# Second-layer chunks regrouped so that each one's output rows lie at one stride and go out in one store

## The chip, the cores and the metric

One core of a Trainium2 chip runs the whole program. The metric is device time in microseconds. The kernel before takes 325.49 us, the median of 3 runs (324.9 to 325.58).

## The reference

Eight batches with 8 heads each, 576 tokens per head, head size 64. A Nystrom attention (32 landmarks, each the mean of 18 consecutive tokens) is followed by two dense layers:

```python
A  = sm(q, k_lm);  Bm = sm(q_lm, k_lm);  C = sm(q_lm, k)
for _ in range(6): Z = 2 * Z - Z @ Bm @ Z
x  = (A @ Z @ C @ v)          # to [4608 tokens, 512]
h  = x @ w_in                 # 512 -> 2048
out = (h * sigmoid(h)) @ w_out  # 2048 -> 512, float32
```

## The kernel before, in words

A planner (class `Plan`) takes operations with priorities, dependencies and estimated durations, simulates the five engines, and writes one fixed order per engine; each engine then runs its list in that order and waits on semaphores. The order comes only from those estimates. SP's list holds the DMA transposes (`qT<-qk` at L479, four per batch from batch 2 on; `ct<-ce` at L717, two per batch from batch 2 on) and all output stores (L871). GpSimd's list issues the loads.

A token of a batch is numbered 18 l + j, with l from 0 to 31 (the landmark it belongs to) and j from 0 to 17. On the chip the 576 tokens of a batch lie as 18 blocks of 32: block x holds the 32 tokens of one j, first all nine even j, then all nine odd j (`jof`, L876: j = 2 (x mod 9) + x div 9). So the tile `etn` (the normalised attention factor, two groups of 128 rows by 576 columns) has its columns in two halves of 288.

Per batch, `layer1` (L789) folds w_in into a matrix `m`, so that the hidden layer is `m` times `etn`: for each of 16 pieces of the hidden dimension two matmuls over 512 token columns (L800) and one Silu on ScalarE into `gm` (L809). The last 64 token columns (blocks 16 and 17, that is j = 15 and 17) go separately: 16 small matmuls per eight pieces (L821) into one bank, and one Silu into `gx` (L831), which collects two batches, 128 tokens.

`layer2` (L842) takes 128 tokens at a time as a chunk: four pieces of four matmuls over w_out into one bank (L850), a copy to one of three buffers `ost` on ScalarE or VectorE (L862), and the store (L864), whose `stores` function issues the DMAs. `layer2_batch` (L879) makes four chunks per batch from `gm` and, after each odd batch, one chunk from `gx` (called the x chunk here). The first matmuls of an attention batch that use `ct`, the transposed third softmax, are at L730 (`cv0`, then `cv1`); at L707 the first two batches make `ct` on TensorE instead.

A store has to write 32 rows per j. In a chunk with j = 0, 2, 4, 6 the destination is 4 pieces by 32 rows by 512 numbers. The third chunk of each batch holds j = 16, 1, 3, 5, which are not at one step, so `stores` issues a DMA of 32 rows and one of 96. The x chunk issues one DMA for each of its two batches, each 2 pieces (j = 15, 17) by 32 rows. That makes five DMAs per batch and two more per pair of batches, 48 in all.

Of the kernel before, what the change touches and what calls it, by code (L numbers as in the profile page):

```python
# [9 lines left out]
AF = mybir.ActivationFunctionType  # L10
# [231 lines left out]
def act_us(n):  # L242
    return 0.06 + 0.00083 * n
# [6 lines left out]
def mm_us(n, count=1):  # L250
    return count * max(n / 2400 + 0.0025, 0.028)
# [3 lines left out]
def kernel(  # L255
# [9 lines left out]
    nc = tc.nc  # L265
    B, H, S, Dh = q.shape
    L = 32
    J = S // L
    JP = J // 2
# [20 lines left out]
    def bank(o, i=0):  # L290
        return banks[o.slot[i]]

    def ring(pool, shape, dt, nm, n):
        return [pool.tile(shape, dt, tag=f"{nm}{i}", name=f"{nm}{i}") for i in range(n)]
# [17 lines left out]
    etn_r = ring(smp, [128, NG, S], BF, "etn", 2)  # L312
# [4 lines left out]
    m_r = ring(smp, [128, NG, DFF], BF, "m", 2)  # L317
# [4 lines left out]
    def mm(out_ap, lhsT, rhs, start=True, stop=True):  # L322
        nc.tensor.matmul(out=out_ap, lhsT=lhsT, rhs=rhs, start=start, stop=stop,  # L323
                         skip_group_check=True)
# [76 lines left out]
    def consts(e):  # L401
# [13 lines left out]
        out=idb, in_=idb, compare_op=OP.is_equal, fill=0.0, base=0, pattern=[[-1, 128]],  # L415
# [371 lines left out]
    l2_last = {}  # L787

    def layer1(b):  # L789
        m_sb, etn = m_r[b % 2], etn_r[b % 2]  # L790
        gm, gx = gm_r[b % 3], gx_r[(b // 2) % 2]
        gm_ops[b], gx_ops[b] = [], []
        pes = []
        for dc in range(NDC):
            cell = {}

            def hm(e, dc=dc, cell=cell):
                ps = bank(cell["o"])
                for g in range(NG):
                    mm(ps, m_sb[:, g, dc * 128:(dc + 1) * 128], etn[:, g, 0:512],  # L800
                       start=(g == 0), stop=(g == 1))
            p = 1000.0 + 100 * b + dc
            o = cell["o"] = A(f"h{dc}.{b}", [("PE", mm_us(512, 2))], hm,
                              etn_ops[b] + m_ops[b, dc // 4] + l2_last.get(("m", b - 3), []), p,
                              psum=1, cls="L1")
            pes.append(o)
            o.unit = b
            gm_ops[b].append(A(f"g{dc}.{b}", [("ACT", act_us(512))],
                               lambda e, dc=dc, cell=cell: nc.scalar.activation(  # L809
                                   out=gm[:, dc, :], in_=bank(cell["o"]), func=AF.Silu),  # L810
                               [o], p, table="silu").reads(o))
            gm_ops[b][-1].unit = b
            if dc % 8 == 7:
                d0 = dc - 7
                cell = {}

                def xm(e, d0=d0, cell=cell):
                    ps = bank(cell["o"]).rearrange("p (c x) -> p c x", c=8)
                    for d in range(8):
                        for g in range(NG):  # L820
                            mm(ps[:, d], m_sb[:, g, (d0 + d) * 128:(d0 + d + 1) * 128],  # L821
                               etn[:, g, 512:576], start=(g == 0), stop=(g == 1))
                o = cell["o"] = A(f"hx{d0}.{b}", [("PE", mm_us(64, 16))], xm,
                                  etn_ops[b] + m_ops[b, dc // 4]
                                  + l2_last.get(("x", b // 2 - 2), []), p + 0.5, psum=1, cls="L1")
                pes.append(o)
                o.unit = b
                c = (b % 2) * 64
                gx_ops[b].append(A(
                    f"gx{d0}.{b}", [("ACT", act_us(512))],  # L830
                    lambda e, d0=d0, cell=cell, c=c: nc.scalar.activation(  # L831
                        out=gx[:, d0:d0 + 8, c:c + 64],
                        in_=bank(cell["o"]).rearrange("p (c x) -> p c x", c=8), func=AF.Silu),
                    [o], p + 0.5, table="silu").reads(o))
                gx_ops[b][-1].unit = b
        l1_done[b] = A(f"l1done.{b}", [("SP", 0.0)], lambda e: None, pes, 0.0, lag=0.0)
# [5 lines left out]
    def layer2(src, deps, prio, stores, split=False):  # L842
        head = [None]
        prev_piece = None
        pieces = []
        for qt in range(4):
            def lm2(e, qt=qt):
                ps = bank(head[0])
                for dc in range(4 * qt, 4 * qt + 4):
                    mm(ps, src(dc), w_out_sb[:, dc, :], start=(dc == 0), stop=(dc == NDC - 1))  # L850
            d = deps(qt) + ([prev_piece] if qt else []) + [wo_ops[qt]]
            d = [(x, 0.0) if x is prev_piece else x for x in d]
            o = A(f"o{qt}@{prio}", [("PE", mm_us(512, 4))], lm2, d, prio + 0.01 * qt,
                  psum=0 if qt else 1, cls="L2")
            if qt == 0:
                head[0] = o
            prev_piece = o
            pieces.append(o)
        i = nost[0] % 3
        nost[0] += 1  # L860
        ost = ost_r[i]
        c = A(f"oc@{prio}", either(512), lambda e: copy(e, ost, bank(head[0])),  # L862
              [prev_piece, ost_st.get(i)], 900.0 + prio / 100).reads(head[0])
        st = A(f"os@{prio}", [("SP", 0.15)], lambda e: stores(ost), [c], prio, dma=0.65, lag=1.6)  # L864
        ost_st[i] = st
        return pieces

    def store_rows(b, js, ost, p0):
        n = len(js)
        step = js[1] - js[0] if n > 1 else 1  # L870
        return nc.sync.dma_start(  # L871
            out=out[b * S:(b + 1) * S, :].rearrange("(l j) n -> j l n", j=J)
            [js[0]:js[-1] + 1:step],
            in_=ost[p0:p0 + n * L, :])

    def jof(blk):  # L876
        return 2 * (blk % JP) + blk // JP

    def layer2_batch(b):  # L879
        l2_last["m", b] = []  # L880
        for c in range(4):
            js = [jof(x) for x in range(4 * c, 4 * c + 4)]

            def stores(ost, js=js):
                i = 0
                while i < 4:
                    n = 1
                    while i + n < 4 and js[i + n] == js[i] + 2 * n:
                        n += 1
                    r = store_rows(b, js[i:i + n], ost, i * L)  # L890
                    i += n
                return r
            l2_last["m", b] += layer2(
                lambda dc, c=c: gm_r[b % 3][:, dc, c * 128:(c + 1) * 128], lambda qt: gm_ops[b][4 * qt:4 * qt + 4],
                5000.0 + 100 * b + 10 * c, stores)
        if b % 2 == 1:
            def stores(ost):
                for bb in range(2):
                    r = store_rows(b - 1 + bb, [jof(16), jof(17)], ost, 64 * bb)
                return r  # L900
            l2_last["x", b // 2] = layer2(
                lambda dc: gx_r[(b // 2) % 2][:, dc, :], 
                lambda qt: [gx_ops[b - 1][qt // 2], gx_ops[b][qt // 2]],
                5000.0 + 100 * b + 40, stores)
# [7 lines left out]
    for b in range(B):  # L912
        attn(b)
        layer1(b)
        layer2_batch(b)
# [4 lines left out]
    with tc.manual_schedule(engines={ET.PE, ET.Activation, ET.DVE, ET.Pool, ET.SP}):  # L920
        table = None
        for o, e, t, end, switch in order:
# [4 lines left out]
            r = o.emit(e)  # L927
# [39 lines left out]
```

## Time and profile before

| | |
|---|---|
| median of 3 runs | 325.49 us |
| the profiled execution, its own time | 326.66 us |
| span of its instructions | 324.9 us |
| mean granted TensorE clock | 0.917 of full speed |
| TensorE matmul busy | 271.2 us (83%) |
| ScalarE busy | 178.1 us (55%) |
| VectorE busy | 97.3 us (30%) |
| GpSimd busy | 106.2 us (33%) |
| chain of waits by engine | PE 48%, DMA 32%, POOL 7%, SP's queue 5% |

Times in the profile's rows are microseconds from the start of the span. PE is TensorE, PEld its weight loads, ACT ScalarE, DVE VectorE, POOL GpSimd, SP the engine that issues transposes and stores; a q behind the name means the engine's instruction queue. "Busy" of PE is not PE at its peak. PEclk is the granted clock as a share of 2.4 GHz, so 0.50 is 1.2 GHz. The DMA share of a stretch is the mean busy share of the core's 16 DMA engines, so 0.125 is two of them; packets still in flight at the end of a short stretch can push it above 1.

### The profile page before, as it was taken

The numbers are of one execution on the slowest core, as the hardware profiler recorded it, in microseconds if no ns is written. First come the engines' busy times: TensorE is split into PE (matmuls) and PEld (weight loads), VectorE is DVE, ScalarE is ACT, GpSimd is POOL, SyncE is SP. The second block draws the span as 40 slices with busy tenths as digits, with TensorE's granted clock in tenths as the row PEclk, the third lists the DMA queues.
The fourth block names the chain that finished last, engine by engine and source line by source line (L and its number), as shares of the span: only waits on it lengthen the run. The fifth ranks groups of instructions, "written<-read, shape, count | busy, mean of one in ns | idle before, by whom it ended". The sixth has DMA issues, their size and how long they took to land.

```text
span 324.9 us, 5951 instructions
## 1 busy us (share of the span) xinstructions
PE 271.2 (83%) x2367; PEld 135.5 (42%) x2367; DVE 97.3 (30%) x258; ACT 178.1 (55%) x405; POOL 106.2 (33%) x133
## 2 busy tenths in 40 slices
PE   7999999669889069998991599979199999999950
PEld 6975554234444034444430345434044544444420
DVE  1685055301736214036460150445125200000000
ACT  1887983838628326984591199835149792111120
POOL 7166249328503570395329222930000000000000
PEclk9999999959999858999996599999669999999995
DMA  6999997894497939787792479778811011322221
GB/s 117 208 200 206 204 209 123 143 202 65 82 155 138 164 62 125 138 148 146 128 217 67 74 136 183 95 95 151 91 32 34 3 32 32 68 68 81 80 76 48
DMA packets 58148, 37.60 MB, mean 116 GB/s; under 512 B 39177, under 2 KB 49417, under 8 KB 58121
## 3 DMA queue, kind: packets, MB, share of 16 engines
q0 software_dynamic: 15232, 18.35, 34.1%
q1 hardware_dynamic: 42888, 18.88, 31.1%
q8 instruction: 18, 0.29, 0.4%
q14 instruction: 10, 0.07, 0.1%
HBM read 36.70 MB, written 9.44 MB: 142 GB/s over the span
## 4 chain that ended last, share of the span: by engine, by line
PE 48%; DMA 32%; POOL 7%; SPq 5%; issue 2%; ACT 1%; DVE 1%; POOLq 0%; ACTq 0%
PE ps L323 48%; DMA ct<-ce 9%; DMA w_in_sb<-in_moe_w_in_dram 6%; DMA qk<-in_k_dram 6%; DMA v<-in_v_dram 6%; DMA qT<-qk 5%; SPq L479 5%; POOL sa L516 2%; POOL qk L368 2%; POOL v L375 1%; POOL sb L516 1%; ACT ce L691 1%; POOL lm L516 1%; DVE etn L667 1%; SPq L717 0%
## 5 line engine op out<-in xcount | busy, mean ns | idle before, releaser
L323 PE MATMUL ps<-w_out_sb,gm 128*128 128x512 bf16 x512 | 122.8, 383 | 0.0
L809 ACT ACTIVATE gm<-ps 128x512 bf16<-128x512 f32 x128 | 67.4, 639 | 33.0 <-PE ps L323 32.8
L323 PE MATMUL ps<-etn,m 128*128 128x64 bf16 (+1 forms) x512 | 75.9, 302 | 0.0
L323 PEld LDWEIGHTS <-gm 128*128 128x128 bf16 x512 | 47.4, 98 | 53.2 <-issue 3.7
L333 ACT COPY ost<-ps 128x512 f32<-128x512 f32 x25 | 14.7, 587 | 58.7 <-PE ps L323 58.6
L323 PEld LDWEIGHTS <-m 128*128 128x128 bf16 x512 | 33.5, 102 | 30.1 <-issue 7.7
L516 POOL TENSOR_TENSOR sa<-qk 128x576 f32<-128x576 bf16 x24 | 30.4, 1286 | 34.7 <-DMA qk<-in_k_dram 34.2
L620 DVE SCALAR_TENSOR_TENSOR st<-st,ps 128x320 bf16<-128x320 bf16 (+3 forms) x54 | 21.6, 408 | 50.9 <-PE ps L323 48.4
L323 PE MATMUL ps<-v,ct 96*64 96x128 bf16 x192 | 10.0, 251 | 18.7 <-DMA ct<-ce 18.7
L516 POOL TENSOR_TENSOR sb<-sa 128x512 f32<-128x512 f32 (+1 forms) x24 | 21.8, 909 | 1.8
L335 DVE CAST m<-ps 128x512 bf16<-128x512 f32 x31 | 19.8, 686 | 8.5 <-PE ps L323 8.4
L368 POOL DMA_DIRECT2D qk<-in_k_dram x8 | 6.0, 747 | 49.9 <-DMA qT<-qk 48.7
L323 PE MATMUL ps<-idb,lm 128*128 128x128 bf16 x32 | 4.6, 235 | 19.0 <-POOL lm L516 18.9
L333 ACT CAST m<-ps 128x512 bf16<-128x512 f32 x33 | 17.9, 616 | 2.6 <-PE ps L323 2.6
L323 PEld LDWEIGHTS <-ct 96*64 96x64 bf16 x192 | 7.1, 126 | 23.2 <-DMA ct<-ce 20.7
L335 DVE COPY ost<-ps 128x512 f32<-128x512 f32 x11 | 7.6, 690 | 29.5 <-PE ps L323 29.5
L375 POOL DMA_DIRECT2D v<-in_v_dram x24 | 14.0, 598 | 5.9 <-DMA w_out_sb<-in_moe_w_out_dram 4.2
L323 PE MATMUL ps<-w_out_sb,gx 128*128 128x512 bf16 x64 | 15.9, 379 | 0.0
L323 PE MATMUL ps<-zer 128*128 128x256 bf16 x95 | 14.9, 301 | 1.1 <-DVE zer L402 1.1
L323 PE MATMUL ps<-st 128*128 128x160 bf16 (+1 forms) x96 | 15.4, 237 | 0.0
L691 ACT ACTIVATE ce<-ps 128x288 bf16<-128x288 f32 x32 | 12.7, 412 | 4.3 <-PE ps L323 4.3
L323 PEld LDWEIGHTS <-st 128*128 128x128 bf16 x96 | 9.4, 104 | 12.4 <-issue 3.8
(68 smaller groups left out, 259.1 us busy)
## 6 DMA issues: line engine op xcount, KB each, us to landing
out_dram<-ost SPq DMA_DIRECT2D x24, 256.0 KB
qk<-in_k_dram POOLq DMA_DIRECT2D x8, 576.0 KB, 9.9
qk<-in_q_dram POOLq DMA_DIRECT2D x8, 576.0 KB, 12.7
v<-in_v_dram POOLq DMA_DIRECT2D x24, 192.0 KB, 13.3
w_out_sb<-in_moe_w_out_dram POOLq DMA_DIRECT2D x4, 512.0 KB, 10.3
out_dram<-ost SPq DMA_DIRECT2D x8, 192.0 KB
w_in_sb<-in_moe_w_in_dram POOLq DMA_DIRECT2D x4, 256.0 KB, 9.0
w_in_sb<-in_moe_w_in_dram POOLq DMA_DIRECT2D x8, 128.0 KB, 7.3
```

The source lines that it names most:

```text
L323: nc.tensor.matmul(out=out_ap, lhsT=lhsT, rhs=rhs, start=start, stop=stop, skip_group_check=True)
L333: nc.scalar.copy(out=out, in_=in_)
L335: nc.vector.tensor_copy(out=out, in_=in_)
L368: lambda e, t=t, src=src: nc.gpsimd.dma_start(out=qk_r[b % 2][:, t].rearrange("p g j d -> p g (j d)"), in_=src[b].rearrange("(g h) (l j) d ...
L375: lambda e, a=a: nc.gpsimd.dma_start(out=v_r[b % 2][a * L:(a + 1) * L, :, :], in_=v[b].rearrange("h (l a x) d -> a l h (x d)", l=L, a=VA)[ ...
L479: lambda e, t=t, g=g: nc.sync.dma_start_transpose(out=qT[:, t, g], in_=qk[:, t, g].rearrange("p j d -> p (j d)")),
L516: lambda e: nc.gpsimd.tensor_tensor(out=o_, in0=a_, in1=b_, op=OP.add),
L620: nc.vector.scalar_tensor_tensor(out=s2[:, g0:g1, lo:SW], in0=s[:, g0:g1, lo:SW], scalar=2.0, in1=ps[:, 0:NG * SW].rearrange("p (g x) -> p ...
L667: nc.vector.tensor_tensor(out=etn[:, g, :], in0=et.rearrange("p c x -> p (c x)"), in1=ln.rearrange("p c x -> p (c x)"), op=OP.mult)
L691: nc.scalar.activation(out=ce[:, :, 0:VP].rearrange("p (i c) (a l) -> p c a i l", c=2, a=VA)[:, c], in_=bank(me[f"C{g}"], c)[:, 0:HS].rear ...
L809: lambda e, dc=dc, cell=cell: nc.scalar.activation(out=gm[:, dc, :], in_=bank(cell["o"]), func=AF.Silu),
```

## The change

The 512 main columns of `etn` are now the first 256 of each half (j = 0, 2, ..., 14 and j = 1, 3, ..., 15), and the remaining 64 columns are the last 32 of each half (j = 16 and 17). The first-layer matmuls therefore read their moving operand in two runs: 2 x 256 columns, and 2 x 32 columns for the small ones, 288 apart. The Silu into `gx` writes the two j of each l next to each other, so that the x chunk holds its tokens in the order batch, l, j. The four main chunks hold j = 0 2 4 6, j = 8 10 12 14, j = 1 3 5 7 and j = 9 11 13 15, each stored by one DMA with a destination of 4 x 32 x 512; the x chunk is stored by one DMA with the destination written as 2 batches x 32 l x 1024 numbers (two neighbouring rows). That makes 36 store DMAs. The planner's estimates, priorities and dependencies are unchanged.

```diff
     def layer1(b):
-        m_sb, etn = m_r[b % 2], etn_r[b % 2]
+        m_sb = m_r[b % 2]
+        etc = etn_r[b % 2].rearrange("p g (c x) -> p g c x", c=2)
...
-                    mm(ps, m_sb[:, g, dc * 128:(dc + 1) * 128], etn[:, g, 0:512],
+                    mm(ps.rearrange("p (c x) -> p c x", c=2),
+                       m_sb[:, g, dc * 128:(dc + 1) * 128], etc[:, g, :, 0:256],
                        start=(g == 0), stop=(g == 1))
...
-                            mm(ps[:, d], m_sb[:, g, (d0 + d) * 128:(d0 + d + 1) * 128],
-                               etn[:, g, 512:576], start=(g == 0), stop=(g == 1))
+                            mm(ps[:, d].rearrange("p (c x) -> p c x", c=2),
+                               m_sb[:, g, (d0 + d) * 128:(d0 + d + 1) * 128],
+                               etc[:, g, :, 256:288], start=(g == 0), stop=(g == 1))
...
-                        out=gx[:, d0:d0 + 8, c:c + 64],
-                        in_=bank(cell["o"]).rearrange("p (c x) -> p c x", c=8), func=AF.Silu),
+                        out=gx[:, d0:d0 + 8, c:c + 64].rearrange("p d (l j) -> p d j l", j=2),
+                        in_=bank(cell["o"]).rearrange("p (d j l) -> p d j l", d=8, j=2),
+                        func=AF.Silu),
...
+    def rows(b, n):
+        return out[b * S:(b + n) * S, :].rearrange("(b l j) n -> b j l n", b=n, j=J)
...
-            js = [jof(x) for x in range(4 * c, 4 * c + 4)]
-            def stores(ost, js=js):
...
+            j0 = 8 * (c % 2) + c // 2
+            def stores(ost, j0=j0):
+                return nc.sync.dma_start(out=rows(b, 1)[0, j0:j0 + 7:2], in_=ost)
...
             def stores(ost):
-                for bb in range(2):
-                    r = store_rows(b - 1 + bb, [jof(16), jof(17)], ost, 64 * bb)
-                return r
+                return nc.sync.dma_start(
+                    out=out[(b - 1) * S:(b + 1) * S, :].rearrange(
+                        "(b l j) n -> b l j n", b=2, j=J)[:, :, J - 2:J].rearrange(
+                            "b l j n -> b l (j n)"), in_=ost)
```

## Rows read from the trace of the kernel before

**Rows 1.** Chain of waits, in order of time: start, us, what.
```profile
82.87 2.79 DMA ct<-ce
...
118.65 13.76 PE ps L323 x137
...
181.05 2.82 DMA ct<-ce
...
207.69 6.21 DMA ct<-ce
...
213.94 10.45 PE ps L323 x96
224.39 10.32 DMA ct<-ce
...
234.75 78.81 PE ps L323 x479
...
313.62 0.59 ACT ost L333
```

**Rows 2.** Timeline of TensorE, 234 to 242 us, idle before in brackets.
```profile
234.75 0.85 PE L323 MATMUL ps<-v,ct 96*64 96x128 bf16 x12 [6.94 <-DMA ct<-ce]
...
241.83 0.53 PE L323 MATMUL ps<-v,ct 96*64 96x128 bf16 x12
```

**Rows 3.** Timeline of SP: start, us, instruction, count.
```profile
120.18 9.80 SPq L479 DMA_TRANSPOSE qT<-qk  x4
...
206.24 1.19 SPq L871 DMA_DIRECT2D out_dram<-ost  x2
...
222.50 1.14 SPq L871 DMA_DIRECT2D out_dram<-ost  x2
224.39 2.28 SPq L717 DMA_TRANSPOSE ct<-ce  x1
226.77 0.99 SPq L871 DMA_DIRECT2D out_dram<-ost  x1
228.80 2.60 SPq L717 DMA_TRANSPOSE ct<-ce  x1
...
314.24 1.14 SPq L871 DMA_DIRECT2D out_dram<-ost  x2
```

**Rows 4.** Stretches: length, busy PE to POOL, PEclk, DMA share, GB/s.
```profile
228.00:230.00 2.00, 0.00 (x0) 0.00 (x0) 0.58 (x3) 0.77 (x4) 0.00 (x0) 1.00 0.13 50
246.60:247.00 0.40, 0.40 (x4) 0.17 (x2) 0.20 (x1) 0.40 (x2) 0.00 (x0) 1.00 0.61 149
286.00:287.00 1.00, 1.00 (x7) 0.41 (x6) 0.00 (x0) 0.00 (x0) 0.00 (x0) 1.00 0.26 102
319.00:323.00 4.00, 0.00 (x0) 0.00 (x0) 0.00 (x0) 0.00 (x0) 0.00 (x0) 0.50 0.13 51
```

**Rows 5.** The same columns, around TensorE's last long wait.
```profile
230.00:231.00 1.00, 0.00 (x0) 0.00 (x0) 0.00 (x0) 0.00 (x0) 0.00 (x0) 0.66 0.55 121
235.00:240.00 5.00, 5.00 (x32) 1.95 (x28) 0.49 (x1) 1.30 (x3) 0.00 (x0) 0.50 0.04 5
```

**Rows 6.** Timeline of SP, single stores of 32 and 96 rows.
```profile
245.76 0.34 SPq L871 DMA_DIRECT2D out_dram<-ost  x1
...
246.16 0.78 SPq L871 DMA_DIRECT2D out_dram<-ost  x1
```

**Rows 7.** Groups by line and form: count, busy us, mean ns, idle before.
```profile
L323 PE MATMUL ps<-qk,idb 128*128 128x128 bf16 x72 | 5.3, 219 | 0.5 <-DMA qk<-in_k_dram 0.5
L323 PE MATMUL ps<-idb,qk 128*128 128x128 bf16 x72 | 5.3, 219 | 0.0
L691 ACT ACTIVATE ce<-ps 128x288 bf16<-128x288 f32 x32 | 12.7, 412 | 4.3 <-PE ps L323 4.3
L648 ACT ACTIVATE et<-ps 128x288 bf16<-128x288 f32 x32 | 11.6, 418 | 4.9 <-PE ps L323 4.8
L831 ACT ACTIVATE gx<-ps 128x512 bf16<-128x512 f32 x16 | 10.0, 645 | 2.1 <-PE ps L323 2.1
```

More of the change, by code (lines that the diff above doesn't have):

```diff
@@ L866, in layer2 @@
         return pieces
[L868 to L877, printed above, removed]
+    def rows(b, n):
+        return out[b * S:(b + n) * S, :].rearrange("(b l j) n -> b j l n", b=n, j=J)
     def layer2_batch(b):
@@ L881, in layer2_batch @@
         for c in range(4):
-            js = [jof(x) for x in range(4 * c, 4 * c + 4)]
-            def stores(ost, js=js):
[L885 to L891, printed above, removed]
-                return r
+            j0 = 8 * (c % 2) + c // 2
+            def stores(ost, j0=j0):
+                return nc.sync.dma_start(out=rows(b, 1)[0, j0:j0 + 7:2], in_=ost)
             l2_last["m", b] += layer2(
@@ L897, in stores @@
             def stores(ost):
-                for bb in range(2):
-                    r = store_rows(b - 1 + bb, [jof(16), jof(17)], ost, 64 * bb)
-                return r
+                return nc.sync.dma_start(
+                    out=out[(b - 1) * S:(b + 1) * S, :].rearrange(
+                        "(b l j) n -> b l j n", b=2, j=J)[:, :, J - 2:J].rearrange(
+                            "b l j n -> b l (j n)"), in_=ost)
             l2_last["x", b // 2] = layer2(
```

## The prediction

> **What bounds the kernel now.** Read the chain of waits first [rows 1]. It ends in 78.81 us of TensorE without a gap from 234.75 us, one copy, and then nothing that any engine does: the copy ends at 314.21 us (313.62 + 0.59), the span at 324.9 us. In front of that TensorE stretch stands a wait of 10.32 us for one transpose of `ct`. So three places are worth a look: the end, that wait, and whether other stores stand on the chain.
>
> The timeline of TensorE says what the wait costs: idle for 6.94 us until 234.75 us [rows 2], so from 227.81 us on. In the chain undisturbed transposes of `ct` land 2.8 us after their issue (three rows, the first and the last shown); this one was issued at 224.39 us [rows 1]. What is special about it stands just ahead of it on SP's timeline: at 222.50 us the two DMAs of an x chunk were issued [rows 3]. The stretches show what these do. From 228 to 230 us the DMA engines are busy to a share of 0.13 and move 50 GB/s: two of the sixteen. At the end, 319 to 323 us, it is again 0.13 and 51 GB/s, and the last issues before it, at 314.24 us, are again an x chunk's [rows 3, 4]. When a chunk of four j is on its way the share is 0.26 (four engines), and while a store of one j runs beside the others it reaches 0.61 [rows 4]. So here a store is spread over as many engines as the outermost count of its destination: two for two j, four for four j, many where the 32 rows come first. An x chunk of 256 KB on two engines takes 262,144 B / 51 GB/s = 5.1 us, and a transpose that needs all sixteen engines waits behind it on two of them. That is why the transpose of 224.39 us is late and why the program ends on a drain. Part of the wait is paid twice: in 230 to 231 us the granted clock averages 0.66, and from 235 to 240 us TensorE works at 0.50 (1.2 GHz) [rows 5] after the idle stretch.
>
> **The change part by part.** I make the sum against the profiled execution, 326.66 us (a span of 324.9 and 1.76 around it), which is 1.17 us over the median of the runs.
>
> *The x chunk's store.* The diff writes its destination as 2 batches x 32 l x 1024 numbers. A batch step is 576 rows, an l step 18 rows, and 576 = 32 x 18: the two levels lie at one stride and fold into 64 steps of 18 rows. They have to, as far as I see: the source is 128 partitions of 512 numbers, so the run of 1024 must be cut in two to match it, and 2 x 32 x 2 x 512 would have four levels, where no DMA of this kernel names more than three. With 64 outermost on one side and 128 on the other, the store can use all sixteen engines: 16 KB on each, 0.64 us at 25.5 GB/s per engine (51 / 2). Four x chunks exist; two of them matter.
>
> *The wait at 224 us.* The x chunk of 222.50 us then takes each engine 0.64 us and not two of them 5.1 us. The transpose of 224.39 us lands after about 2.8 us, at 227.2 us, before TensorE runs dry at 227.81 us. Ends: all 6.94 us gone, or, if the x chunk's share still stands ahead of it (0.64 us for its data and as much for a slow start), some 0.7 us left. I take 6.7.
>
> *The clock after it.* With no idle stretch the clock should stay up. The five microseconds at 0.50 [rows 5] hold 2.5 us of work at full speed, so 2.5 us come back; ends 0 (another idle stretch drops it as well) and 2.8 (with the rise in the next microsecond).
>
> *What is late next.* The second transpose (issue 228.80 us) can't start earlier, as its source is written only by then. Ahead of it stands the chunk store of 226.77 us, now issued about a microsecond sooner, since the transpose before it no longer holds SP for 2.28 us [rows 3]. TensorE needs the second `ct` 7.08 us after the first (234.75 to 241.83) [rows 2], some 4.6 us at full clock, so at about 232.4 us. The landing: undisturbed 231.6; behind a four-engine store, as at 207.69 us, where a store issued 1.45 us ahead made it 6.21 [rows 1, 3], counted 7.7 us from the store's issue at about 225.7: 233.4. Between them I charge 0.7 us; ends 0 and 2.
>
> *The end.* Today the x chunk's rows queue on two engines, at 80 ns per row of 2 KB (2048 B / 25.5 GB/s) 64 rows each. Spread, each engine has 8: 56 fewer, 4.5 us less. Two rows per engine less from the third chunk's former 32-row store and its earlier end on SP add a little: 4.6. Ends: 3.0, if the spread store starts slowly on the four engines that the main chunks still hold, and 5.1, its whole time.
>
> *The third chunk of each batch.* One store of 4 x 32 replaces 0.34 us and 0.78 us of SP's time [rows 6] by about 0.55 us (half of the 1.14 us of two stores issued back to back [rows 3], four or two j alike). Its rows per engine stay at 32 (96 rows on three engines, 128 on four). Where SP or the store is ahead of a transpose on the chain, at 206.24 us before the one of 207.69 us [rows 1, 3], data start about 0.4 us sooner; TensorE waits there until 213.94 us, so I take 0.4. Elsewhere SP waits for data and the saving is nothing.
>
> *The x chunk after batch 1.* The four transposes of `qT` at 120.18 us take 9.80 us [rows 3]; they will be shorter. TensorE works without a gap through that time (13.76 us from 118.65 us [rows 1]), which hides it, so I count nothing. If they helped the later loads too, that would be a gain.
>
> *First-layer matmuls with two runs.* The two forms with 128 columns compare directly: the landmark sums read two runs of 64 columns and take 219 ns, the transposes with one run of 128 also take 219 ns [rows 7]. Cost zero; the upper end is 5 ns on each of 512 matmuls, 2.6 us.
>
> *The Silu into `gx`.* It writes 2-byte numbers at a step of 4 bytes. The nearest row, the exponential into `ce`, writes runs of 32 scattered over the tile and takes 412 ns against 418 for the plain one into `et` [rows 7]. Zero; the upper end is a doubling of 645 ns, 16 times, 10.3 us if nothing hid it. No row shows a step of two. The Trainium skill, "SBUF — State Buffer", section "SBUF: two separate sides", has accesses within one 16-byte line at full bandwidth, by which a step of 4 bytes is free; no run here shows it.
>
> *Sum:* 6.7 + 2.5 - 0.7 + 4.6 + 0.4 = 13.5 us. The profiled execution would be 313.2 us, the median 312.0 us.
>
> **A rule that speaks against it.** The rows show two, four and many engines for outermost counts of two, four and 32 [rows 4]. The Trainium skill, "DMA: Bandwidth & Descriptors", section "Why a DMA increments its semaphore by 16 and not by 1", says that the engines used are the largest number up to 16 that divides the slowest dimension of both sides, as the instruction carries it. The trace agrees (0.13 is 2/16, 0.26 is 4/16). But taken on the destination as the diff writes it, with 2 outermost, it gives two engines again and a time of 325.
>
> **The rivals.**
>
> *A. The forecast:* 312.0 us.
>
> *B. The next wait eats part of it.* The chunk store of 226.77 us still uses four engines, and the second transpose stands behind it. If that lands at 235 us, TensorE idles 2.6 us at about 232.4 us, and the clock falls again: 1.9 us more than charged and the 2.5 us of clock are lost, 13.5 - 4.4 = 9.1, so 316.4 us. For it: the four-engine store ahead of the transpose of 207.69 us. Against: the clock was still 1.00 in 228 to 230 us, in the first two microseconds of today's idle stretch [rows 4].
>
> *C. It does not do what it says:* the x chunk's levels are not folded, it stays on two engines, now as one DMA of 128 rows. The main chunks have four j before and after. Then only 0.4 us at 207 us and a few tenths at the end are won: 325.0 us. For it: the order in which the diff writes the levels. Against: the four levels.
>
> *D. Slower:* the Silu into `gx`, on ScalarE, with a step of two. Behind it in ScalarE's order stand the next Silus and copies, which free TensorE's banks. Its price is 16 times its extra time. Against 13.5 us it decides from 0.84 us more each (2.3 times 645 ns); at 1.0 us more the total is 16.0 - 13.5 = 2.5 us slower, 328.0 us. For it: no row has such a step. Against: the `ce` row.
>
> **How the numbers follow.** A 0.66, B 0.16, C 0.12, D 0.06. The range reaches from the ends of A (all of 6.94, 2.8, 5.1, 0.4 and no second wait, 15.2 us, 310.3, and a little for the loads that might come sooner) past B towards C: 309 to 321 us; C and D, 0.18, lie outside. About 0.2% (0.65 us) is what a measurement of this kernel can tell from no change. A, B and a little of C are faster, 0.83; most of C is the same, 0.10; D and a remnant of C slower, 0.07.
>
> **What would show it.** Step by step: a DMA share at the end that never sits at 0.13 for four microseconds, and the span ending some 6 us after the last store's issue, not 10.7; TensorE's wait before the first `ct` after the second x chunk under 1 us and a clock of 1.00 behind it; a wait of about 0.7 us before the second; Silus into `gx` at 645 ns and first-layer matmuls as long as before; 36 stores at about 0.55 us. A share of 0.13 over the x chunks makes C true and the forecast wrong; a long wait before the second `ct` makes B true.

## The result, and the profile after

The changed kernel takes 314.77 us (median of 4 runs, 313.94 to 315.49) against 325.53 us before (4 runs, 324.9 to 327.26): a ratio of 0.966, 95% interval 0.9616 to 0.9704. The forecast was 312.0. Here and below a ratio compares the runs in the usual, faster state with such runs of the kernel before on the same chip, while the medians are over all runs, so the two can differ a little. The profiled execution takes 314.78 us, with a span of 313.0 us and a mean granted clock of 0.937 (0.917 before).

The chain of waits, in order of time, from 160 us (start, us, what):

```profile
161.68 19.59 DMA v<-in_v_dram
...
210.08 5.65 DMA ct<-ce
...
215.78 13.94 PE ps L323 x147
...
230.63 3.96 DMA ct<-ce
...
234.63 9.24 PE ps L323 x90
...
243.88 62.58 PE ps L323 x342
...
306.53 0.59 ACT ost L333
```

The piece of 10.32 us [rows 1] is gone. TensorE's timeline has the two places where `ct` is used:

```profile
229.91 0.53 PE L323 MATMUL ps<-v,ct 96*64 96x128 bf16 x12 [0.27 <-DMA ct<-ce]
...
234.63 0.53 PE L323 MATMUL ps<-v,ct 96*64 96x128 bf16 x12
```

Idle for 0.27 us before the first, where it was 6.94 [rows 2], and not at all before the second. SP's timeline at the same place and at the end:

```profile
224.49 0.58 SPq L887 DMA_DIRECT2D out_dram<-ost  x1
226.22 1.23 SPq L717 DMA_TRANSPOSE ct<-ce  x1
227.49 0.56 SPq L881 DMA_DIRECT2D out_dram<-ost  x1
230.63 1.22 SPq L717 DMA_TRANSPOSE ct<-ce  x1
...
307.14 0.57 SPq L887 DMA_DIRECT2D out_dram<-ost  x1
```

One issue for the x chunk instead of two, and a transpose that holds SP for 1.23 us, not 2.28 [rows 3]. The stretches (length, busy PE to POOL, PEclk, DMA share, GB/s) show the x chunk of 224.49 us, the clock behind the old wait, and the last drain:

```profile
224.50:226.50 2.00, 2.00 (x38) 0.80 (x44) 0.90 (x5) 1.44 (x8) 0.00 (x0) 1.00 1.04 259
226.50:229.50 3.00, 3.00 (x51) 0.98 (x27) 2.78 (x6) 2.38 (x5) 0.00 (x0) 1.00 0.45 83
235.00:240.00 5.00, 5.00 (x35) 2.50 (x30) 3.33 (x6) 4.32 (x8) 0.00 (x0) 1.00 0.11 40
307.20:309.00 1.80, 0.00 (x0) 0.00 (x0) 0.00 (x0) 0.00 (x0) 0.00 (x0) 1.00 0.33 113
309.00:311.00 2.00, 0.00 (x0) 0.00 (x0) 0.00 (x0) 0.00 (x0) 0.00 (x0) 1.00 0.55 192
311.00:312.20 1.20, 0.00 (x0) 0.00 (x0) 0.00 (x0) 0.00 (x0) 0.00 (x0) 0.66 0.09 32
```

No drain of an x chunk sits at 0.13 for microseconds any more [rows 4]: while the last x chunk drains the share reaches 0.55 and 192 GB/s, and the span ends 5.86 us after its issue (10.66 before). The clock is 1.00 from 235 to 240 us, where it was 0.50 [rows 5]. Last, the groups by form (count, busy us, mean ns, idle before):

```profile
L323 PE MATMUL ps<-etn,m 128*128 128x512 bf16 x256 | 68.3, 403 | 0.1
L834 ACT ACTIVATE gx<-ps 128x512 bf16<-128x512 f32 x16 | 12.2, 787 | 1.9 <-PE ps L323 1.8
L323 PE MATMUL ps<-etn,m 128*128 128x64 bf16 x256 | 10.1, 196 | 0.0
```

The Silu into `gx` takes 787 ns where it took 645 [rows 7]; the first-layer matmuls with two runs are as long as before (405 and 199 ns then).

The trace also records how each store is laid out and in how many parts it lands, and that bears out the numbers of engines read off the DMA share. In the kernel before a store recorded as 2 x 32 rows lands in 2 parts, 3 x 32 in 3, 4 x 32 in 4 (leaving out one early event of each), and one of 32 rows in 16. The changed x chunk is recorded as 64 x 2 rows and lands in 16 parts, the last x chunk from 310.07 to 312.11 us. Every transpose lands in 16 parts, in both kernels.

The spans' difference, 11.9 us, lies in four places: up to the first `ct` multiplication after the 207 us transpose 1.84 us later (213.94 to 215.78); the idle time at the next one 6.67 us less; from there to the end of the last matmul 78.81 against 76.55 us, 2.26 less; from the last store's issue to the end 4.80 less. 1.84 - 6.67 - 2.26 - 4.80 = -11.89.

### The profile page after: what moved, and what is told of

It reads as the page before. It is cut to its first block, busy times and chain, and to the rows that moved or that the text cites. A ratio compares the mean times of both kernels' runs of the same rounds, so it can differ in the third digit from the quotient of the medians.

```text
span 313.0 us, 5933 instructions
## 1 busy us (share of the span) xinstructions
PE 269.5 (86%) x2367; PEld 135.0 (43%) x2367; DVE 96.6 (31%) x258; ACT 179.7 (57%) x405; POOL 106.9 (34%) x133
## 4 chain that ended last, share of the span: by engine, by line
PE 52%; DMA 29%; ACT 6%; POOL 4%; SPq 3%; issue 2%; DVE 2%; POOLq 0%; ACTq 0%
PE ps L323 52%; DMA v<-in_v_dram 11%; DMA ct<-ce 7%; DMA w_in_sb<-in_moe_w_in_dram 7%; SPq L479 3%; ACT gm L811 3%; DMA qT<-qk 3%; POOL qk L368 2%; POOL v L375 2%; ACT gx L834 1%; ACT L914 1%; DVE bbd L576 1%; ACT ce L691 0%; DVE bm L570 0%; POOL lm L516 0%
```

## The experiments

The theory (T): the gain comes from the x chunk's rows lying on sixteen DMA engines instead of two, at two places, and the regrouping of the main chunks gives nothing. Its rival R1: fewer and larger stores are what pays.

**The changed kernel again**, as the base for the three after it.

> The changed kernel once more, on the chip of the three runs sent with it. All theories: 314 to 315.5 us. It gives the base for the differences of the others.

316.24 us, a little over the expected 314 to 315.5, against 326.3 us for the kernel before on this chip, ratio 0.9698 (0.9656 to 0.9741). It reached the 214 us multiplication at 216.24 us.

**The spread alone.** The kernel before, with the x chunk's store split by j:

```diff
                 for bb in range(2):
-                    r = store_rows(b - 1 + bb, [jof(16), jof(17)], ost, 64 * bb)
+                    for i in range(2):
+                        r = store_rows(b - 1 + bb, [jof(16 + i)], ost, 64 * bb + 32 * i)
```

> The kernel before with one edit: the x chunk goes out as four DMAs of 32 rows instead of two of 64, so that 32 stands outermost in each. Nothing is regrouped, 56 store DMAs instead of 48. Theory T (the gain comes from the x chunk's rows lying on all sixteen engines instead of two): the 6.9 us wait before the first ct at 224 us and the 5 us drain go as in the changed kernel, 311 to 315 us. Rival R1 (the gain comes from fewer and larger stores, all of 128 rows): 325 us or a little more, since there are more and smaller ones. If the strided Silu into gx costs the changed kernel the 1.8 us by which it reached the 214 us wait later (theory G), this kernel, with the plain Silu, is 1 to 2.5 us faster than the changed one; if not (rival L, the later transfers fell badly), it is within 0.7 us of it or slower by the longer issue of four DMAs.

316.79 us, ratio 0.9729 (0.9686 to 0.9772): the whole gain within the intervals, with eight stores more instead of twelve fewer. R1 falls. The time is above the expected 311 to 315 us, on a chip on which the changed kernel was above its range too. The plain Silu (644 ns) does not make it faster than the changed kernel, and it reached the 214 us multiplication at 216.06 us, so theory G finds no support; L is not shown by that either.

**The x chunk put back on two engines**, main chunks regrouped:

```diff
-                return nc.sync.dma_start(out=out[...].rearrange("b l j n -> b l (j n)"), in_=ost)
+                for bb in range(2):
+                    r = nc.sync.dma_start(out=rows(b - 1 + bb, 1)[0, J - 2:J],
+                                          in_=ost[64 * bb:64 * bb + 64, :])
```

> The changed kernel with the x chunk alone put back: the plain Silu into gx (order j, l) and two stores of 2 x 32 rows, j = 16 and 17. The main chunks stay regrouped, one store of 128 rows each; 40 store DMAs. Theory T: the share of 0.13 over the x chunks is back, 324 to 326 us. Rival R1 (regrouping the main chunks, 32 and 96 rows into one store of 128, gives a good part): 316 to 322 us.

327.89 us, a little over the expected 324 to 326, ratio 1.0027 (0.9988 to 1.0066): no change. The stores of 128 rows in the main chunks alone are worth nothing. Its timeline of TensorE has the wait back, its stretch at the end the low share:

```profile
236.50 0.85 PE L323 MATMUL ps<-v,ct 96*64 96x128 bf16 x12 [3.29 <-DMA ct<-ce]
```
```profile
319.00:324.00 5.00, 0.00 (x0) 0.00 (x0) 0.00 (x0) 0.00 (x0) 0.00 (x0) 0.50 0.15 57
```

**The order made by the moving operand** instead of the Silu:

```diff
-                            mm(ps[:, d].rearrange("p (c x) -> p c x", c=2),
+                            mm(ps[:, d].rearrange("p (x c) -> p x c", c=2),
...
-                               etc[:, g, :, 256:288], start=(g == 0), stop=(g == 1))
+                               etc[:, g, :, 256:288].rearrange("p c x -> p x c"),
+                               start=(g == 0), stop=(g == 1))
```

> The changed kernel with the order l, j of the x chunk made by the moving operand of the 256 small first-layer matmuls (columns taken alternately from the two halves) instead of by the Silu, which writes gx plainly again. Theory G (the strided write made the Silu into gx 142 ns longer, 16 times, and ScalarE stands on the chain near 130 to 142 us): the Silu is back at 645 ns and the time 1 to 2.3 us under the changed kernel's, if the matmuls stay at 196 ns. Rival L: within 0.5 us of the changed kernel. If the alternating read slows the small matmuls, by x ns each, 0.26 us per ns come on top at most.

321.21 us, ratio 0.9857 (0.9805 to 0.9908), 5 us slower than the changed kernel. The groups point to the cause: the Silu is short again, but the 256 small matmuls are busy 18.2 us instead of 10.1.

```profile
L323 PE MATMUL ps<-etn,m 128*128 128x64 bf16 x256 | 18.2, 224 | 0.0
L835 ACT ACTIVATE gx<-ps 128x512 bf16<-128x512 f32 x16 | 9.6, 601 | 6.3 <-PE ps L323 6.2
```

So this run could not tell G from L; it priced a worse place for the same reordering.

**The kernel before, a second profile.**

> The kernel before once more, for a second profile of it. The changed kernel, the spread alone and the two-engine version all came to the first ct multiplication of the 214 us wait at 215.8 to 217.6 us, the profiled execution before at 213.94. Theory N (the early profile of before was lucky by about 2 us, executions of one kernel differ by that much ahead of this point): 215 to 217.5 us here, with a wait of 6 to 8 us before 235 to 238 us and a span of 325 to 328. Rival U (every one of the edits costs 2 us ahead of that point): 213.5 to 214.5 us again.

The 214 us multiplication began at 214.88 us, between the two theories' ranges, nearer N. The wait after it (4.44 us, until 233.19 us) and the span (323.3 us) were under N's ranges, so one execution more decides for neither. What it does show is that the wait is not the same length each time:

```profile
214.88 0.53 PE L323 MATMUL ps<-v,ct 96*64 96x128 bf16 x12 [1.82 <-DMA ct<-ce]
233.19 0.85 PE L323 MATMUL ps<-v,ct 96*64 96x128 bf16 x12 [4.44 <-DMA ct<-ce]
```

**Only the last x chunk spread, only the second one spread** (the split of the first diff under `b == 7` or `b == 3`).

> The kernel before with only the last x chunk (after batch 7) spread, as four DMAs of 32 rows. Theory T with two separate places: the drain alone goes, 4 to 5 us under the kernel before on the same chip, a ratio of 0.984 to 0.988; the wait near 235 us stays at 5 to 7 us. Rival (the gain is one thing, a shorter store queue in all the last third): half or more of the whole gain, a ratio under 0.982.

322.14 us, ratio 0.9904 (0.9868 to 0.9941): 0.96% of 326 us is 3.1 us, a little under the expected 4 to 5. The wait stayed, at 3.86 us, shorter than the expected 5 to 7:

```profile
234.81 0.85 PE L323 MATMUL ps<-v,ct 96*64 96x128 bf16 x12 [3.86 <-DMA ct<-ce]
```

> The kernel before with only the second x chunk (after batch 3) spread, as four DMAs of 32 rows. Theory T: the wait near 235 us falls under 1 us, TensorE's stretch behind it runs at a clock of 1.00 instead of 0.50, and the drain of 10.7 us stays: 6 to 9 us under the kernel before, a ratio of 0.972 to 0.982. Rival (the wait is the four-engine store's, not the x chunk's): no change, 0.995 to 1.005.

319.51 us, ratio 0.9835 (0.977 to 0.9899): 5.4 us (3.3 to 7.5 by the interval), also under what was expected. The wait is gone and so is the low clock:

```profile
229.29 0.53 PE L323 MATMUL ps<-v,ct 96*64 96x128 bf16 x12 [0.29 <-DMA ct<-ce]
```
```profile
235.00:240.00 5.00, 5.00 (x30) 2.52 (x29) 3.17 (x7) 4.32 (x8) 0.00 (x0) 1.00 0.14 45
```

Together 0.96% + 1.65% = 2.6%, against the 2.7% of all four spread: within the intervals the two places are separate and make up the gain.

**All chunks spread.** If two engines hurt, four may as well. VectorE writes the columns of `etn` with l outside, so every store has 32 or 64 rows outermost:

```diff
-                nc.vector.tensor_tensor(out=etn[:, g, :], in0=et..., in1=ln..., op=OP.mult)
+                for c in range(2):
+                    nc.vector.tensor_tensor(
+                        out=etn[:, g, 256 * c:256 * c + 256].rearrange(
+                            "p (q l i) -> p q i l", q=2, i=4),
+                        in0=et[:, c, 0:256]..., in1=ln[:, c, 0:256]..., op=OP.mult)
...
+                return nc.sync.dma_start(
+                    out=rows(b, 1)[0, j0:j0 + 7:2].rearrange("j l n -> l j n"), in_=ost)
```

> All chunks l-major: VectorE writes the columns of etn so that each chunk's tokens run over l outside and its four (or two) j inside; first-layer matmuls read one run again, the Silu into gx is plain, and every store has 32 or 64 outermost, so every store can use sixteen engines; 36 stores. VectorE's product into etn becomes three instructions instead of one. Theory T carried on (engines per store is what matters): the ct pairs behind a main store land in 3 to 4 us instead of 5.5, the end follows the last issue by some 3.5 us instead of 5.9; 308 to 313 us. Rival (VectorE's strided writes cost more than that, 0.2 us and more for each of 16, with the chain through etn): 314 to 320 us. Rival R2 (only the two-engine stores hurt, four engines are enough): 314 to 317 us with the same waits as the changed kernel.

288.58 us, ratio 0.8843 (0.8776 to 0.891). The direction was expected, the size was not: 26 to 28 us below the changed kernel's two medians, not 2 to 8. If the stores did this, four-engine stores held up something larger than the drain and the `ct` pairs. Two kernels without the new order test it.

**All stores as DMAs of 32 rows; only the main chunks so** (the loop in `stores` that joins neighbouring j is taken out; the x chunk split as above, or left alone):

```diff
-                    while i + n < 4 and js[i + n] == js[i] + 2 * n:
-                        n += 1
```

> The kernel before with every store split into DMAs of 32 rows, one for each j: 144 store DMAs instead of 48, nothing regrouped, VectorE's product into etn as before. Theory T2 (the all-spread kernel's 37 us come from its stores leaving engines 0 to 3 free for the loads and transposes, which need all sixteen): 285 to 295 us, even though SP issues three times as many DMAs (0.33 us each, four in a row 1.5 us against 0.55). Rival R1 (fewer, larger stores are what pays): 325 to 335 us. Rival V (the gain came from VectorE's new order of etn's columns and not from the stores): 313 to 318 us, as with the x chunk spread alone.

292.17 us, ratio 0.8922 (0.8877 to 0.8967), with 144 stores. It is the stores, not VectorE's order, and three times as many of them. The landing of the loads (size of one, median us from issue to landing) in the changed kernel and then here:

```profile
qk<-in_k_dram POOLq DMA_DIRECT2D x8, 576.0 KB, 9.4
qk<-in_q_dram POOLq DMA_DIRECT2D x8, 576.0 KB, 12.3
v<-in_v_dram POOLq DMA_DIRECT2D x24, 192.0 KB, 13.3
```
```profile
qk<-in_k_dram POOLq DMA_DIRECT2D x8, 576.0 KB, 6.4
qk<-in_q_dram POOLq DMA_DIRECT2D x8, 576.0 KB, 8.6
v<-in_v_dram POOLq DMA_DIRECT2D x24, 192.0 KB, 10.4
```

The chain of the changed kernel holds two loads of `v`, the one of 19.59 us shown above and the first one here; the chain of this kernel holds only the second one here:

```profile
99.78 15.76 DMA v<-in_v_dram
```
```profile
96.91 9.71 DMA v<-in_v_dram
```

and TensorE's waits, those of the changed kernel first (total, times, longest), shrink:

```profile
PE ps L323 <- POOL lm L516: 16.5, 5, 5.4
PE ps L323 <- DMA ct<-ce: 14.7, 5, 5.9
```
```profile
PE ps L323 <- POOL lm L516: 11.0, 3, 4.9
PE ps L323 <- DMA ct<-ce: 4.5, 3, 2.5
```

The main chunks are 32 x 256 KB; on four engines at 25.5 GB/s each that is, as an estimate, 82 us of each of the four (8.39 MB / 4 / 25.5 GB/s), which the loads and transposes then share. The two waits above make up 15.7 of the 21.4 us between the two spans (313.0 and 291.6 us). A rival would be that the buffers `ost` come free sooner; but in the traces of the kernel before and the changed one none of TensorE, ScalarE, VectorE and GpSimd waits for a store.

> The same with the x chunk left as in the kernel before, on two engines: only the main chunks are split into DMAs of 32 rows. Theory T2: the loads and transposes gain as with all of them split; the drain at the end and the transposes behind the second x chunk stay late, so 5 to 10 us slower than all split: 292 to 302 us. Rival (the x chunks were all that mattered, the main chunks' split adds only issues): 324 to 330 us.

305.07 us, ratio 0.931 (0.9258 to 0.9362): 13 us behind all split, more than the 5 to 10 expected. The x chunk on two engines costs more here than in the kernel before (2.7%, some 9 us); why stays open.

**VectorE's write made contiguous, its reads stepped** (the all-spread kernel with the patterns of both sides exchanged).

> The all-spread kernel with VectorE's product into etn walking the output in order and reading its two inputs at a step of 32, instead of writing at a step of four numbers (940 ns for 256 columns there, 26.9 us in all, and about 9 us of the chain of waits). If the strided write is what makes it slow: 300 to 450 ns for 256 columns and 281 to 287 us. If any stride costs the same: no change, 287 to 291 us.

288.83 us, ratio 0.8854 (0.8809 to 0.89): no change. A step costs on either side; the rows are the kernel before's (576 columns without a step), the all-spread kernel's, then this one's:

```profile
L667 DVE TENSOR_TENSOR etn<-et,ln 128x576 bf16<-128x576 bf16 x16 | 13.1, 821 | 2.8 <-ACT ln L662 2.8
```
```profile
L668 DVE TENSOR_TENSOR etn<-et,ln 128x256 bf16<-128x256 bf16 x32 | 26.9, 940 | 1.7 <-ACT ln L662 1.7
```
```profile
L668 DVE TENSOR_TENSOR etn<-et,ln 128x256 bf16<-128x256 bf16 x32 | 23.8, 786 | 1.7 <-ACT ln L662 1.7
```

**A version meant to beat both kernels, the one before and the changed one.** In a half of 288 columns ordered l, j (even j or odd j), column n is output row 2 n or 2 n + 1, so any 128 neighbours lie at one step. The exponential into `et` makes that order, writing at a step for one group of rows (the first lines below) and reading at a step for the other; nothing else is stepped:

```diff
-                          out=et[:, c], in_=bank(...)[:, 0:HS], func=AF.Exp, ...
+                    out=et[:, c].rearrange("p (l i) -> p i l", l=L),
+                    in_=bank(...)[:, 0:HS].rearrange("p (i l) -> p i l", l=L), ...
...
+                    out=et[:, c].rearrange("p (l i) -> p l i", l=L),
+                    in_=bank(...)[:, 0:HS].rearrange("p (i l) -> p l i", l=L), ...
...
+        return out[b * S:(b + 1) * S, :].rearrange("(n c) d -> c n d", c=2)[c, n0:n0 + n]
```

> A version to beat both: the exponential into et (128 x 288, 32 instructions, 418 ns each before) puts the tokens of each half in the order l, j, so that column n of a half is output row 2 n or 2 n + 1. Every main chunk is then 128 rows at one step of two rows, one store whose outermost count is 128; the x chunk goes out in four DMAs of 32 rows with a plain Silu; VectorE's product into etn is one contiguous instruction again; first-layer matmuls read two runs as in the changed kernel. One half of the exponentials writes at a step, the other reads at a step, so that both prices show. Theory T2 (engines per store): loads, transposes and drain as in the two kernels with all stores spread; without VectorE's 22 us more of strided work and without 144 issues, 282 to 288 us if the exponentials stay under 500 ns. Rival (a step on ScalarE costs as on VectorE, a microsecond and more each): 288 to 300 us.

288.03 us, ratio 0.8827 (0.8782 to 0.8872). It beats both, but is level with the all-spread kernel within the intervals. The time is just outside the expected 282 to 288, whose condition (under 500 ns) half of the exponentials miss, and at the edge of the rival's range. The spread holds (the `qk` loads land in 5.7 and 8.8 us), and the two ways to step on ScalarE come out far apart:

```profile
L648 ACT ACTIVATE et<-ps 128x288 bf16<-128x288 f32 x16 | 21.8, 1611 | 2.8 <-PE ps L323 2.8
L654 ACT ACTIVATE et<-ps 128x288 bf16<-128x288 f32 x16 | 6.0, 433 | 0.1
```

Line 648 writes at a step of nine numbers, line 654 reads PSUM at a step of 32. With all of them reading, 16 x (1611 - 433) ns = 18.8 us would come off ScalarE, and line 648 is 7.0% of this kernel's chain. That is an estimate; the version was not run.

## Why the prediction was right

*The x chunk's store.* Right. The two levels fold: the instruction is recorded with 64 x 2 rows and lands in 16 parts. The share of 0.13 is gone, and the spread without the regrouping gives the gain. The rule of the Trainium skill ("DMA: Bandwidth & Descriptors", "Why a DMA increments its semaphore by 16 and not by 1") goes by the pattern as the instruction carries it. The trace agrees (2, 3, 4 and 16 parts for 2, 3, 4 and 32 or more outermost), once it is taken on that folded pattern and not on the order in which the diff writes the levels. Rival C is out.

*The wait.* In the profiled pair 6.67 us against the forecast's 6.7. That size belonged to one execution. In the four profiles with the second x chunk on two engines the 214 us multiplication begins at 213.94, 214.88, 215.51 and 217.62 us, and the wait after it is 6.94, 4.44, 3.86 and 3.29 us: an execution that is early there waits longer. So the agreement of 6.67 with 6.7 is partly luck. Taken alone the place is worth 5.4 us, clock included, and not the 8.5 of its three terms (6.7 + 2.5 - 0.7). This is the term that was mis-sized most; with the other misses below it is enough for the 2.8 us by which the forecast was below the measured median, but the intervals are too wide to share these out.

The mechanism was right, and the trace shows it more sharply than the prediction put it: the transpose does not wait on two engines only. In these four profiles none of its sixteen parts lands before the x chunk's last one, and the first lands 0.7 us after that (230.79 and 231.48 us in the kernel before). The trace also shows what was odd in the profiled execution. Fourteen parts had landed by 231.63 us, and the last came 3.1 us later, at 234.71, beside the four-engine store of 226.77 us; in the other three profiles the last part came 0.9 us after the fourteenth. So some 2.2 us of the 6.94 belong to that one execution; why its last part was so late is not shown.

*The clock and what is late next.* The clock came back. The second transpose, charged 0.7 us, cost nothing: it landed at 234.59 us (3.96 us after its issue), as TensorE came to it. The two terms together, a gain of 2.5 - 0.7 = 1.8 us, measured 2.26. Rival B is out. The delay that it and this term were priced from (206.24 us) was no four-engine store: the two stores there are the third chunk's, 32 rows in 16 parts and 96 rows in 3.

*The end.* 4.80 us in the profiles against the forecast's 4.6; alone it gave 3.1 us (1.9 to 4.3 by the interval).

*The third chunk of each batch.* The forecast had 0.4 us less at 207 us; the profiles show 1.84 us more up to that place. In the profiled pair this is the miss that took the forecast's 13.5 us to 11.9. Four executions of kernels that are alike up to there (the two of before and the ones with only the second or the last x chunk spread) reached it at 213.94, 214.88, 215.13 and 215.51 us, so 0.9 us of the 1.84 is that the profiled execution was early. Against their mean, 214.87, the two of the changed kernel (215.78 and 216.24) are 1.1 us late and the spread-only kernel's (216.06) 1.2; what causes that stays open, and the four lie 1.6 us apart among themselves. The regrouping as such gave nothing (1.0027).

*The Silu into `gx`.* The forecast took zero; it is 142 ns more for each of 16, 2.3 us of ScalarE. The nearest row, runs of 32, was too far from a step of two. The Trainium skill ("SBUF — State Buffer", "SBUF: two separate sides") would have a step of 4 bytes free; 787 against 645 ns says otherwise, and the measurement decides. The extra did not show in the time: the spread-only kernel without it is no faster. Rival D had the right place, but the price is a sixth of what would have decided (0.14 against 0.84 us).

*The two-run matmuls, and the x chunk after batch 1.* Zero as forecast for the former, 403 and 196 ns. The latter's transposes were counted as hidden, and the gains of the second and the last x chunk alone add up to that of all four within the intervals.

What the prediction did not see is that the row of 0.26 for the main chunks was the same disease: it took that as the normal state and asked only what the x chunk cost. Spreading those as well was worth some 25 us more (316.79 to 292.17 us).

## What to carry to other kernels

Read the DMA share while a store drains alone: here 0.13 and 0.26 were two and four of sixteen engines, and the cure was the order of the destination's levels (many rows outermost, or levels that fold), not fewer or larger DMAs. Here stores on a few engines cost less at their own end (3.1 us for the last x chunk) than in the loads and transposes that ran beside them, so price them by those landings too. If tokens must be reordered for it, try first to let ScalarE read PSUM at a step instead of writing or multiplying at one, and compare a wait over several executions before its full length goes into a sum.

## What the runs showed of the hardware that was not expected

- ScalarE: writing 2-byte numbers at a step of 4 bytes took 787 ns against 645 for 128 x 512, and at a step of 18 bytes 1611 ns against 418 for 128 x 288 [rows 7]. Reading PSUM at a step of 128 bytes took 433 ns.
- VectorE: a product of 256 columns written at a step of 8 bytes took 940 ns, with stepped reads (64 bytes) instead 786 ns; without a step 576 columns took 821 ns.
- TensorE: 256 matmuls of 64 columns whose moving operand alternates between two places were busy 18.2 us; in two runs 10.1 us.
- DMA: a transpose issued behind a store on two engines landed none of its sixteen parts until that store had ended, and the first part 0.7 us after it, in four profiles.
- 144 stores of 64 KB beat 48 of 64 to 256 KB by 34.5 us. The order of the rows decides here and not the size: 36 stores of 256 KB, spread, came to 288.58 us.
